# First block's entry: weight transfers issued earlier, column sums on TensorE, second group five units behind, attention's vector work first

## The chip, the cores and the metric

The kernel runs on one core of a Trainium2 chip. The time is device microseconds of one execution. The profile is of one execution; the times of the kernel before are of separate runs. In the rows PE is the matrix engine (TensorE), PEld its weight loads, DVE is VectorE, ACT is ScalarE, POOL is GpSimd, SP issues most of the transfers.

## The reference, cut to what matters

```python
# attention: B=4, 8 heads, 768 positions, head size 64; chunks of 32 queries,
# 16 keys to the left, 8 to the right, 8 memory tokens
a = np.exp(scores - max); a = a / (a.sum() + 1e-9); out = a @ v_full
x = out as [3072, 512]                  # 24 token tiles of 128
# first block (moe_*): one wide layer, d_ff = 2048
h = x @ w_in                            # 512 x 2048
r = np.maximum(h, 0.0)
g = s * (r * r) + b
x = g @ w_out                           # 2048 x 512
# second block (moe2_*): 8 experts, 384 tokens each, dealt out greedily by sorted gate logits
logits = x @ w_gate; ...; out[mask] = np.maximum(x[mask] @ w1[e], 0.0) @ w2[e]
```

Since g = s·r² + b, the first block is x2 = s·(r² @ w_out) + b·(sum of w_out over its 2048 rows). The kernel computes r² @ w_out and adds b times the column sums of w_out at the end of each tile; these column sums are what one part of the change moves to another engine.

## The kernel before, in words

Attention runs by token tile t (24 of them): `load_q`, `load_k`, `load_v` issue transfers, `k_transpose` and `stages` do the work (transposes pk and pq, scores sc, softmax on DVE and ACT, transposes pp, products po, the division `xr`, transposes px, and a split of the result into a rounded half and a remainder, `xT0` and `xT1`, kept for a group).

The first block runs by group j of two token tiles (256 columns) and by f, one of 16 slices of d_ff. One unit (j,f) is `gemm1` (12 products of 128x256 into a PSUM tile ph), then ACT's relu, square and rounding, then DVE's subtraction that leaves the remainder (line 324), then `gemm2` (6 products of 128x512 into the group's two accumulators). `gemm2` stands LAG = 3 units behind `gemm1`. The list `units` sets which unit follows which: ten units of group 0 first, then one of group 1 and one of group 0 in turn, then the rest of group 1, then groups 2 to 11 one after another.

The weights w_in and w_out of the first block arrive as 64-bit floats and are made into 32-bit ones on the chip, in 32 tiles of 128x512 (even numbers are slices of w_in, odd ones of w_out; the order is 0, 2, 4, 1, 6, 3, 8, 5 and so on). `convert` does one tile: a transfer of 512 KB into `raw` (3 buffers), ACT's y (line 277), DVE's u (278), u (280) and y (281), and in `split` ACT's rounding (262) and POOL's remainder (263). y and u have two buffers each. For a tile of w_out POOL then adds y into `wsum` (line 290). `load_wg`, between groups 1 and 2, multiplies a matrix of ones with wsum (pws, line 397), which sums over the partitions.

`begin` and `startup` write the order of SP's transfers by hand, and `begin` also that of TensorE. On the other engines, and later on TensorE too, a scheduler arranges the instructions when the kernel is built, in an order that then stands; each engine runs its own list in that order, and waits at an instruction until what it needs is there. A tile of w_in must be converted before `gemm1` of its f, one of w_out before `gemm2` of its f, and xT of group 1 must be there before any unit (1,f).

## Time and profile before

| | |
|---|---|
| median of 3 runs | 1113.73 us (1112.22 to 1116.49) |
| the profiled execution | 1110.14 us |
| its span | 1108.4 us |
| PE busy | 1017.7 us, 92% of the span |
| DVE busy | 776.3 us, 70% |
| ACT busy | 474.1 us, 43% |
| POOL busy | 230.9 us, 21% |

The span runs from the first to the last recorded instruction, and the execution's own time is 1.7 us longer. Busy shares are averages over stages with different limits: in the first 145 us the weights are converted while units already run, and from there to about 660 us the first block runs on. A row of the timeline gives an instruction's start, its length, engine, line, operation and the tiles it writes and reads; in square brackets stands the idle time before it and what ended that.

### The profile page before, as it was taken

How to read it: one execution, taken by the hardware profiler on the slowest of the kernel's cores; microseconds unless marked ns; L12 is line 12 of the kernel's file. 1: busy time of each engine (PE TensorE's matmuls, PEld its weight loads, DVE VectorE, ACT ScalarE, POOL GpSimd, SP SyncE). 2: the span in 40 equal slices, each digit the busy share in tenths (PEclk: the TensorE clock that was granted, in tenths of full speed). 3: DMA queues.
4: the chain of work that ended last, by engine and by line, in shares of the span. 5: the costliest groups of instructions: out<-in, count | busy, mean ns of one | idle time of the engine just before them, and what ended most of it. 6: DMA issues, size and time to landing. Idle time of an engine off the chain costs nothing.

```text
span 1108.4 us, 25066 instructions
## 1 busy us (share of the span) xinstructions
PE 1017.7 (92%) x9397; PEld 889.8 (80%) x9397; DVE 776.3 (70%) x2979; ACT 474.1 (43%) x1055; POOL 230.9 (21%) x257
## 2 busy tenths in 40 slices
PE   4678899999999999999999999958989899987997
PEld 3557788888888898989898888747878787877986
DVE  4898846984889598989698643579677667774210
ACT  4656554444444454545444445034244143333421
POOL 2566530000121011121120000010112020135631
PEclk9989999999999999999999998959999899998999
DMA  7966503121212121212211000144346063353500
GB/s 168 229 185 167 132 19 127 46 71 38 54 23 73 37 66 47 50 36 62 58 37 37 1 1 20 51 149 153 113 126 202 18 200 95 116 144 113 161 29 29
DMA packets 157913, 96.56 MB, mean 87 GB/s; under 512 B 100312, under 2 KB 141272, under 8 KB 157664
## 3 DMA queue, kind: packets, MB, share of 16 engines
q1 hardware_dynamic: 153376, 81.32, 27.2%
q0 software_dynamic: 3840, 12.59, 3.5%
q8 instruction: 74, 1.21, 0.5%
q10 hardware_dynamic: 576, 1.05, 0.3%
q14 instruction: 47, 0.39, 0.1%
HBM read 82.33 MB, written 12.60 MB: 86 GB/s over the span
## 4 chain that ended last, share of the span: by engine, by line
PE 63%; DVE 21%; issue 7%; DMA 5%; ACT 1%; POOL 1%; SPq 1%; POOLq 0%; DVEq 0%; ACTq 0%
PE ph L316 19%; PE o L345 19%; PE pg L910 8%; PE pf L889 7%; DVE lsc L378 5%; DVE e L839 4%; PE pc L708 2%; DVE u L280 2%; DMA raws<-in_moe_w_dram 2%; DVE g L324 1%; PE po L221 1%; PE sc L195 1%; DVE y L281 1%; DVE rounded L795 1%; PE px L870 1%
## 5 line engine op out<-in xcount | busy, mean ns | idle before, releaser
L316 PE MATMUL ph<-xT,win 128*128 128x256 f32 x2304 | 323.7, 288 | 10.0 <-ACT win L262 7.2
L316 PEld LDWEIGHTS ph<-xT,win 128*128 128x128 f32 x2304 | 301.6, 192 | 28.4 <-ACT win L262 10.6
L345 PE MATMUL o<-wout,g 128*128 128x512 f32 x1038 | 275.0, 400 | 4.4 <-DVE g L324 2.2
L345 PEld LDWEIGHTS o<-wout,g 128*128 128x128 f32 x1038 | 184.4, 189 | 39.4 <-DVE g L324 3.4
L378 DVE SCALAR_TENSOR_TENSOR lsc<-x,wgb 128x128 int8<-128x128 f32 x640 | 158.3, 299 | 3.3 <-DMA wgb<-wgd 1.1
L319 ACT ACTIVATE r<-ph 128x256 f32<-128x256 f32 x192 | 72.9, 382 | 172.0 <-PE ph L316 160.6
L889 PE MATMUL pf<-xgh,e 128*128 128x384 f32 x512 | 140.8, 349 | 0.0
L910 PE MATMUL pg<-e,hh 128*128 128x512 f32 x384 | 130.5, 415 | 0.0
L838 ACT ACTIVATE e<-raws 128x512 fp32r<-128x512 f32 x128 | 79.6, 630 | 93.8 <-DMA raws<-in_moe_w_dram 92.8
L324 DVE TENSOR_TENSOR g<-r,g 128x256 fp32r<-128x256 f32 x173 | 80.2, 465 | 53.7 <-ACT g L323 50.9
L889 PEld LDWEIGHTS pf<-xgh,e 128*128 128x128 f32 x512 | 96.5, 196 | 5.1 <-issue 3.0
L378 DVE SCALAR_TENSOR_TENSOR lsc<-c,wgb 128x512 int8<-128x512 f32 x128 | 98.9, 773 | 2.1
L910 PEld LDWEIGHTS pg<-e,hh 128*128 128x128 f32 x384 | 74.5, 198 | 19.1 <-issue 5.5
L889 PE MATMUL pf<-xgl,e 128*128 128x384 f32 x256 | 88.7, 346 | 0.0
L897 DVE SCALAR_TENSOR_TENSOR hl<-pf,hh 128x384 fp32r<-128x384 f32 x64 | 35.3, 553 | 69.0 <-ACT hh L896 69.0
L320 ACT ACTIVATE r<-r 128x256 f32<-128x256 f32 x192 | 79.7, 418 | 5.4
L910 PE MATMUL pg<-e,hl 128*128 128x512 f32 x192 | 79.4, 414 | 0.0
L323 ACT ACTIVATE g<-r 128x256 fp32r<-128x256 f32 x173 | 71.6, 416 | 5.0 <-PE o L345 0.3
L859 POOL DMA_INDIRECT xg<-x2d,vw x24 | 24.7, 1030 | 200.1 <-DVE vw L702 127.2
L917 POOL DMA_INDIRECT out_dram<-qk,vw x24 | 25.6, 1068 | 186.8 <-ACT qk L916 174.6
L839 DVE TENSOR_TENSOR e<-raws,e 128x512 fp32r<-128x512 f32 x96 | 60.2, 682 | 3.4 <-PE pg L910 1.3
L896 ACT ACTIVATE hh<-pf 128x384 fp32r<-128x384 f32 x64 | 30.9, 485 | 71.6 <-PE pf L889 70.2
(216 smaller groups left out, 1358.2 us busy)
## 6 DMA issues: line engine op xcount, KB each, us to landing
raws<-in_moe_w_dram SPq DMA_DIRECT2D x128, 256.0 KB
vw<-in_v_dram SPq DMA_DIRECT2D x176, 56.0 KB
raw<-in_moe_w_in_dram SPq DMA_DIRECT2D x16, 512.0 KB
raw<-in_moe_w_out_dram SPq DMA_DIRECT2D x16, 512.0 KB
k<-in_k_dram SPq DMA_DIRECT2D x24, 256.0 KB
q<-in_q_dram SPq DMA_DIRECT2D x24, 256.0 KB
x2d<-x SPq DMA_DIRECT2D x20, 256.0 KB
wgb<-wgd SPq DMA_DIRECT2D x1, 2048.0 KB
```

The costliest lines, as they stand in the source:

```text
L316: nc.tensor.matmul(ph, win_ap(a, kk, f), x[:, kk, :], start=(n == 0), stop=(n == 3 * KD - 1))
L319: nc.scalar.activation(r, ph, AF.Relu)
L320: nc.scalar.activation(r, r, AF.Square)
L323: nc.scalar.activation(hi, r, AF.Copy)
L324: nc.vector.tensor_tensor(lo, r, hi.bitcast(F32), op=ALU.subtract)
L345: nc.tensor.matmul(PO[j][u], g[:, u * P:(u + 1) * P], wout_ap(a, f), start=(f == 0 and n == 0), stop=(f == FT - 1 and n == 2))
L378: nc.vector.scalar_tensor_tensor(sc[:, z], a[:, z], 1.0, b[:, z], op0=ALU.mult, op1=ALU.mult, accum_out=acc[:, i:i + 1])
L838: nc.scalar.activation(hi, raw, AF.Copy)
L839: (V if ph < E - 2 else nc.gpsimd).tensor_tensor(lo, raw, hi.bitcast(F32), op=ALU.subtract)
L889: nc.tensor.matmul(pf, w[:, kk, f * P:(f + 1) * P], x[:, kk, :], start=(n == 0), stop=(n == 3 * KD - 1))
L897: V.scalar_tensor_tensor(lo, pf, 0.0, hi.bitcast(F32), op0=ALU.max, op1=ALU.subtract)
L910: nc.tensor.matmul(pg, h[:, j * P:(j + 1) * P], w[:, f, :], start=(n == 0), stop=(n == 3 * FT2 - 1))
```

## The change

Five things are changed, all before group 3. First, the transfers of the first three slices of w_in are issued earlier: the first before the memory tokens, the second before v of tile 0, the third between v of tiles 0 and 1. Second, POOL's clearing of wsum and its 16 additions are gone; TensorE multiplies a matrix of ones with both halves of each slice of w_out, 32 products of 128x512 into a PSUM tile psw (`column_sums`, two behind each `gemm2` of group 0), and the product with ones in `load_wg` is gone. Third, group 1 starts behind five units of group 0 and not ten. Fourth, the two PSUM banks that ph had until group 3 become one, `halves`, whose two halves are used in turn, and one for psw. Fifth, the DVE and ACT instructions of attention tiles 0 to 3 are marked as urgent for the scheduler. The conversions, which were all handed to the scheduler before the first unit, are now handed over two by two, ahead of each unit of group 0.

```diff
@@ -56,7 +56,6 @@
     b_col = const.tile([P, 1], F32, name="b_col")
     L = const.tile([P, E, NTILE], F32, name="L")
     wsum = const.tile([P, DM], F32, name="wsum")
-    nc.gpsimd.memset(wsum, 0.0)
 
     def bigw(shape, name):
         return big.tile([P] + shape, F32R, tag="w", name=name)
@@ -105,6 +104,20 @@
                                 mk[:B * M, 2 * hp:2 * hp + 2, :].rearrange("p h d -> p (h d)"),
                                 ident[:B * M, :B * M])
         nc.vector.tensor_copy(memkT.rearrange("p h b m -> p h (b m)"), pm[:, :, :B * M])
+
+    class Ahead:
+
+        def __init__(self, engine):
+            self.engine = engine
+
+        def __getattr__(self, name):
+            def call(*args, **kw):
+                with tc.high_priority():
+                    return getattr(self.engine, name)(*args, **kw)
+            return call
+
+    def engines(t):
+        return (Ahead(nc.vector), Ahead(nc.scalar)) if t < 2 * GT else (nc.vector, nc.scalar)
 
     vb = [None, None]
     q_raw, k_raw, kT, xT = {}, {}, {}, {}
@@ -152,21 +165,23 @@
                                           ap=[[D, r1 - r0], [2 * S * D, HP], [1, D]]))
 
     def k_transpose(t):
+        V, S = engines(t)
         x = k_raw.pop(t)
         pk = psa[0].tile([P, HP, P], F32, tag="pa", name=f"pk{t}")
         for hp in range(HP):
             nc.tensor.transpose(pk[:, hp, :], x[:, 2 * hp:2 * hp + 2, :].rearrange("p h d -> p (h d)"), ident)
         kT[t] = at.tile([P, HP, P], F32, tag="kT", name=f"kT{t}", bufs=3)
-        nc.scalar.activation(kT[t], pk, AF.Copy)
+        S.activation(kT[t], pk, AF.Copy)
 
     def windows(t):
...
@@ -257,10 +273,24 @@
 
     sctx = ExitStack()
     st = sctx.enter_context(tc.tile_pool(name="st", bufs=2))
+    onesr = st.tile([P, P], F32R, name="onesr", bufs=1)
+    nc.vector.tensor_scalar(onesr, ident, 0.0, 1.0, op0=ALU.mult, op1=ALU.add)
 
     def split(c, hi, lo, i):
         nc.scalar.activation(hi, c, AF.Copy)
         nc.gpsimd.tensor_tensor(lo, c, hi.bitcast(F32), op=ALU.subtract)
+
+    raws = {}
+
+    def fetch(src, a, n, i):
+        raw = st.tile([P, a, n, 2], I32, tag="raw", name=f"raw{i}", bufs=3)
+        nc.sync.dma_start(raw.rearrange("p a f w -> p a (f w)"),
+                          src.bitcast(I32).rearrange("(a p) f -> p a f", p=P))
+        return raw
+
+    def fetch_win(f):
+        if w_in.dtype != F32:
+            raws[2 * f] = fetch(w_in[:, f * P:(f + 1) * P], KD, P, 2 * f)
 
     def convert(src, a, n, hi, lo, i):
 
@@ -269,9 +299,7 @@
             nc.sync.dma_start(c, src.rearrange("(a p) f -> p a f", p=P))
             split(c, hi, lo, i)
             return c
-        raw = st.tile([P, a, n, 2], I32, tag="raw", name=f"raw{i}", bufs=3)
-        nc.sync.dma_start(raw.rearrange("p a f w -> p a (f w)"),
-                          src.bitcast(I32).rearrange("(a p) f -> p a f", p=P))
+        raw = raws.pop(i) if i in raws else fetch(src, a, n, i)
         y = st.tile([P, a, n], F32, tag="y", name=f"y{i}")
         u = st.tile([P, a, n], I32, tag="u", name=f"u{i}")
         nc.scalar.activation(y, raw[:, :, :, 1].bitcast(F32), AF.Copy, scale=2.0 ** -112)
@@ -286,8 +314,11 @@
         convert(w_in[:, f * P:(f + 1) * P], KD, P, win_ap3(0, f), win_ap3(1, f), 2 * f)
 
     def load_wout(f):
-        y = convert(w_out[f * P:(f + 1) * P, :], 1, DM, wout_ap3(0, f), wout_ap3(1, f), 2 * f + 1)
-        nc.gpsimd.tensor_tensor(wsum, wsum, y[:, 0, :], op=ALU.add)
+        convert(w_out[f * P:(f + 1) * P, :], 1, DM, wout_ap3(0, f), wout_ap3(1, f), 2 * f + 1)
+
+    def column_sums(f):
+        for a in range(2):
+            nc.tensor.matmul(psw[0], onesr, wout_ap(a, f), start=(f + a == 0), stop=(f == FT - 1 and a == 1))
 
     G = {}
 
@@ -307,8 +338,14 @@
             kept.append([k[:, 0], k[:, 1]])
         return (x[:, f % 4 + (4 if f >= 12 else 0), :] for x in kept[-1])
 
+    ps_h, half = None, [0]
+
     def gemm1(j, f):
-        ph = ps_h.tile([P, GN], F32, tag="ph", name=f"ph{j}_{f}")
+        if ps_h is None:
+            half[0] ^= 1
+            ph = halves[:, half[0], :]
+        else:
+            ph = ps_h.tile([P, GN], F32, tag="ph", name=f"ph{j}_{f}")
         xh, xl = xT[j]
         n = 0
         for kk in range(KD):
@@ -331,11 +368,11 @@
             pass
 
     def gemm2_(j, f):
-        nonlocal ps_o, ps_l
+        nonlocal ps_h, ps_o, ps_l
         if (j, f) == (3, 0):
             octx.close()
-            ps_o, ps_l = (actx.enter_context(tc.tile_pool(name=n, bufs=k, space=PSUM, reuse_waits="tile"))
-                          for n, k in (("ps_o3", 3), ("ps_l", 1)))
+            ps_h, ps_o, ps_l = (actx.enter_context(tc.tile_pool(name=n, bufs=k, space=PSUM, reuse_waits="tile"))
+                                for n, k in (("ps_h", 2), ("ps_o3", 3), ("ps_l", 1)))
         if f == 0:
             PO[j] = [ps_o.tile([P, DM], F32, tag="po", name=f"o{j}_{u}") for u in range(GT)]
         hi, lo = G.pop((j, f))
@@ -391,11 +428,7 @@
         nc.vector.tensor_tensor(wog[:, f, E:2 * E], wf, wog[:, f, 0:E].bitcast(F32), op=ALU.subtract)
 
     def load_wg():
-        ones = xp[0].tile([P, P], F32, tag="x2", name="onesP")
-        nc.vector.memset(ones, 1.0)
-        ps = psa[0].tile([P, DM], F32, tag="pa", name="pws")
-        nc.tensor.matmul(ps, ones, wsum, start=True, stop=True)
-        nc.vector.tensor_scalar(wsum, ps, b_col, None, op0=ALU.mult)
+        nc.vector.tensor_scalar(wsum, psw[0], b_col, None, op0=ALU.mult)
         wg[0] = xp[0].tile([P, E, DM], F32, tag="wgb", name="wgb", bufs=1)
         wgd = dram.tile([E, DM], F32, name="wgd")
         wr[0] = xp[0].tile([P, KD, E], F32, name="wr", bufs=1)
@@ -425,6 +458,7 @@
         load_q(0)
         load_k(1)
         k_transpose(1)
+        fetch_win(0)
         for i in range(2):
             load_mem(i, 0, nc.gpsimd.tensor_copy)
             vb[i] = 0
@@ -434,7 +468,9 @@
         next(run0)
         load_q(1)
         load_k(2)
+        fetch_win(1)
         load_v(0)
+        fetch_win(2)
         k_transpose(2)
         next(run1)
         load_v(1)
@@ -461,15 +497,17 @@
         with tc.manual_schedule(engines={mybir.EngineType.PE}):
             begin()
         ps_s.close()
-        psa[0], ps_h, ps_o = (
+        psa[0], ps_o, ps_w = (
             c.enter_context(tc.tile_pool(name=n, bufs=k, space=PSUM, reuse_waits="tile"))
-            for n, k, c in (("ps_a", 2, ctx), ("ps_h", 2, actx), ("ps_o", 4, octx)))
+            for n, k, c in (("ps_a", 2, ctx), ("ps_o", 4, octx), ("ps_w", 1, octx)))
+        psw = [ps_w.tile([P, DM], F32, name="psw")]
+        halves = ps_w.tile([P, 2, GN], F32, name="halves")
         startup()
-        feed(len(convs))
     gp = actx.enter_context(tc.tile_pool(name="gp", bufs=4, side="right", reuse_waits="tile"))
-    units = [(0, f) for f in range(10)]
+    SKEW = 5
+    units = [(0, f) for f in range(SKEW)]
     for f in range(FT):
-        units += [(1, f)] + ([(0, f + 10)] if f + 10 < FT else [])
+        units += [(1, f)] + ([(0, f + SKEW)] if f + SKEW < FT else [])
     units += [(j, f) for j in range(2, NG) for f in range(FT)]
     wog = twice = ps_l = wsum_g = None
 
@@ -506,11 +544,16 @@
             if i >= 4 * FT and i % 6 == 3 and gated < FT:
                 through_gate(gated)
                 gated += 1
+            if j == 0:
+                feed(2)
             gemm1(j, f)
             if j * FT + f < LATE:
                 pend.append((j, f))
             if pend and (len(pend) > LAG or j * FT + f >= LATE):
-                gemm2(*pend.pop(0))
+                gemm2(*pend[0])
+                z = pend.pop(0)
+                if z[0] == 0:
+                    column_sums(z[1])
             if j >= NG - 2 and f:
                 if f == 1:
                     twice = wr[0][0:2 * E, 0, :]
```

The first list is DVE's, at the place where xT of group 1 is completed (xT1_1<-px3, tile 3). u and y with a number are the conversions' tiles by that number, g1 is the remainder that `gemm2` needs, by group and f; a number behind the name only tells buffers apart. Before:

```order
L280 SCALAR_TENSOR_TENSOR u15_858<-y15_857,u15_858 128x512
L324 TENSOR_TENSOR g10_8_1227<-r0_8_1223,g00_8_1226 128x256
L281 SCALAR_TENSOR_TENSOR y15_857<-y15_857,u15_858 128x512
L280 SCALAR_TENSOR_TENSOR u20_869<-y20_868,u20_869 128x512
L241 TENSOR_TENSOR xT1_1_609<-px3_754,xT1_0_608 128x4x128
L278 TENSOR_SCALAR u17_879<-raw17_876 128x512
L281 SCALAR_TENSOR_TENSOR y20_868<-y20_868,u20_869 128x512
L278 TENSOR_SCALAR u22_890<-raw22_887 128x512
```

And in the changed kernel, where lines 278, 280, 281 and 324 have become 306, 308, 309 and 361, and line 116 is the wrapper of the urgent instructions:

```order
L116 TENSOR_TENSOR xr3_748<-po3_0_713,den3_747 128x4x64
L116 TENSOR_TENSOR xr3_748<-po3_1_714,den3_747 128x4x64
L308 SCALAR_TENSOR_TENSOR u17_1018<-y17_1017,u17_1018 128x512
L309 SCALAR_TENSOR_TENSOR y17_1017<-y17_1017,u17_1018 128x512
L308 SCALAR_TENSOR_TENSOR u22_1082<-y22_1081,u22_1082 128x512
L306 TENSOR_SCALAR u19_1092<-raw19_1089 128x512
L116 TENSOR_TENSOR xT1_1_610<-px3_754,xT1_0_609 128x4x128
L309 SCALAR_TENSOR_TENSOR y22_1081<-y22_1081,u22_1082 128x512
```

Before, tiles 17 and 22 begin behind this instruction; now tile 17 is done ahead of it, tile 22 lacks only its last step, and tile 19 has begun. The remainders of nine units of group 0 stand ahead of it before, and of five now.

The second list is DVE's at the end of the conversions, the last step of tile 31. Before:

```order
L206 TENSOR_REDUCE mx5_1682<-sc5_0_1647 128x4
L241 TENSOR_TENSOR xT2_1_1609<-px4_1603,xT2_0_1608 128x4x128
L207 TENSOR_TENSOR sm5_1681<-sc5_0_1647,mx5_1682 128x4x64
L280 SCALAR_TENSOR_TENSOR u31_1006<-y31_1005,u31_1006 128x512
L324 TENSOR_TENSOR g10_15_1840<-r0_15_1836,g00_15_1839 128x256
L324 TENSOR_TENSOR g11_6_1866<-r1_6_1862,g01_6_1865 128x256
L281 SCALAR_TENSOR_TENSOR y31_1005<-y31_1005,u31_1006 128x512
L205 MEMSET sc5_1_1648 32x4x8
```

And in the changed kernel:

```order
L308 SCALAR_TENSOR_TENSOR u29_1717<-y29_1716,u29_1717 128x512
L309 SCALAR_TENSOR_TENSOR y29_1716<-y29_1716,u29_1717 128x512
L308 SCALAR_TENSOR_TENSOR u31_1727<-y31_1726,u31_1727 128x512
L361 TENSOR_TENSOR g10_8_1261<-r0_8_1257,g00_8_1260 128x256
L309 SCALAR_TENSOR_TENSOR y31_1726<-y31_1726,u31_1727 128x512
L361 TENSOR_TENSOR g11_4_1286<-r1_4_1282,g01_4_1285 128x256
L361 TENSOR_TENSOR g10_9_1333<-r0_9_1329,g00_9_1332 128x256
L221 MEMSET sc5_0_1616 32x4x8
L222 TENSOR_REDUCE mx5_1651<-sc5_0_1616 128x4
```

Before, the remainders of 16 units of group 0 and 7 of group 1 stand ahead of the last step of tile 31, 23 in all; now it is 9 of group 0 and 4 of group 1, 13 in all, and the scores' maxima of tile 5 and the second half of xT2 stand behind it.

The third list is TensorE's, where group 1 begins (win and wout are the weights' halves, o the accumulators of `gemm2`, ph or halves the result of `gemm1`). Before:

```order
L345 MATMUL o0_1_1099<-wout00_78,g10_6_1175 128x512
L235 MATMUL px3_754<-ident_64,xr3_748 128x128 x4
L158 MATMUL pk5_1494<-ident_64,k5_1482 128x128 x4
L316 MATMUL ph0_9_1236<-xT0_0_420,win11_77 128x256
L316 MATMUL ph0_9_1236<-xT0_0_420,win01_75 128x256
...
L316 MATMUL ph0_9_1236<-xT0_0_420,win11_77 128x256
L316 MATMUL ph1_0_1262<-xT1_0_608,win00_74 128x256
L186 MATMUL pq4_1501<-ident_64,q4_1472 128x128 x4
L345 MATMUL o0_0_1098<-wout00_78,g00_7_1200 128x512
```

And in the changed kernel:

```order
L237 MATMUL po3_1_714<-vw1_95,pT3_711 32x65
L321 MATMUL psw_461<-wout10_79,onesr_106 128x512
L321 MATMUL psw_461<-wout00_77,onesr_106 128x512
L321 MATMUL psw_461<-wout10_79,onesr_106 128x512
L251 MATMUL px3_754<-ident_64,xr3_748 128x128 x4
L172 MATMUL pk5_1463<-ident_64,k5_1451 128x128 x4
L353 MATMUL halves_462<-xT1_0_609,win00_73 128x256
L321 MATMUL psw_461<-wout01_78,onesr_106 128x512
...
L353 MATMUL halves_462<-xT1_0_609,win10_75 128x256
L321 MATMUL psw_461<-wout11_80,onesr_106 128x512
L211 MATMUL sc4_0_1483<-kwin0_96,qT4_1475 32x64
```

Between units (0,4) and (1,0) there is now no `gemm1`, only products for psw and attention; before, unit (0,9) stands directly ahead of unit (1,0). From here on the changed list has `gemm2` one unit behind `gemm1` until group 3, and all 32 products for psw stand ahead of unit (1,6).

## Rows read from the trace of the kernel before

**Rows 1.** Windows of the span, one row a stretch; header first.

```profile
core 0: us, PE busy (x) PEld busy (x) DVE busy (x) ACT busy (x) POOL busy (x), PEclk, DMA share, GB/s
...
24.88:38.85 13.97, 3.79 (x16) 3.05 (x17) 12.20 (x27) 7.26 (x12) 6.52 (x5) 1.00 0.96 256
38.85:88.20 49.35, 39.75 (x454) 33.24 (x453) 45.01 (x74) 31.73 (x68) 30.13 (x23) 0.90 0.75 198
88.20:145.05 56.85, 50.51 (x471) 41.12 (x471) 50.05 (x69) 32.60 (x77) 36.98 (x32) 1.00 0.48 131
145.05:169.46 24.41, 24.41 (x212) 21.22 (x211) 7.89 (x21) 11.77 (x30) 4.80 (x7) 1.00 0.10 21
169.46:250.00 80.54, 80.28 (x867) 70.93 (x865) 69.37 (x463) 36.97 (x89) 3.81 (x13) 1.00 0.30 84
```

**Rows 2.** Chain of waits, 0 to 240 us: start, length, what.

```profile
20.27 8.92 DMA raw<-in_moe_w_out_dram
...
112.04 1.71 DVE u L280
...
132.64 1.97 PE ph L316 x14
...
161.35 1.40 PE o L345 x6
162.74 1.44 PE ph L316 x12
...
178.14 0.79 PE sc L195 x53
```

**Rows 3.** DVE by line, 0 to 168 us: busy us, mean ns, idle before.

```profile
L280 DVE SCALAR_TENSOR_TENSOR u<-y,u 128x512 int32<-128x512 int32 x32 | 34.3, 1071 | 9.7 <-ACT y L277 9.5
L281 DVE SCALAR_TENSOR_TENSOR y<-y,u 128x512 int32<-128x512 int32 x32 | 28.7, 896 | 1.5 <-DVE den L228 0.4
L278 DVE TENSOR_SCALAR u<-raw 128x512 int32<-128x512 int32 x32 | 23.3, 729 | 7.7 <-DMA raw<-in_moe_w_in_dram 6.4 <-DMA raw<-in_moe_w_out_dram 1.0
L324 DVE TENSOR_TENSOR g<-r,g 128x256 fp32r<-128x256 f32 x31 | 19.2, 630 | 12.5 <-ACT g L323 12.5
```

**Rows 4.** POOL timeline around 57 us: start, length, instruction.

```profile
56.70 1.46 POOL L290 TENSOR_TENSOR wsum<-wsum,y 128x512 f32<-128x512 f32 x1
58.12 1.46 POOL L263 TENSOR_TENSOR wout<-y,wout 128x512 fp32r<-128x512 f32 x1
```

**Rows 5.** DVE timeline around 60 us, the same columns.

```profile
56.94 1.50 DVE L278 TENSOR_SCALAR u<-raw 128x512 int32<-128x512 int32 x1
58.36 1.77 DVE L280 SCALAR_TENSOR_TENSOR u<-y,u 128x512 int32<-128x512 int32 x1
60.24 0.69 DVE L281 SCALAR_TENSOR_TENSOR y<-y,u 128x512 int32<-128x512 int32 x1
...
60.98 0.42 DVE L278 TENSOR_SCALAR u<-raw 128x512 int32<-128x512 int32 x1
...
63.67 0.41 DVE L324 TENSOR_TENSOR g<-r,g 128x256 fp32r<-128x256 f32 x1
```

**Rows 6.** ACT by line, first step of a conversion.

```profile
L277 ACT ACTIVATE y<-raw 128x512 f32<-128x512 f32 x32 | 21.4, 668 | 9.8 <-DMA raw<-in_moe_w_in_dram 4.5 <-POOL wout L263 2.9 <-POOL win L263 2.4
```

**Rows 7.** DVE timeline where the two groups' xT and the conversions end.

```profile
37.36 0.68 DVE L241 TENSOR_TENSOR xT<-px,xT 128x512 fp32r<-128x512 f32 x1
...
87.53 0.68 DVE L241 TENSOR_TENSOR xT<-px,xT 128x512 fp32r<-128x512 f32 x1
...
144.22 0.83 DVE L281 SCALAR_TENSOR_TENSOR y<-y,u 128x512 int32<-128x512 int32 x1
```

**Rows 8.** SP timeline: v of tiles 0 and 1.

```profile
9.34 8.88 SPq L150 DMA_DIRECT2D vw<-in_v_dram  x16
```

**Rows 9.** PE timeline between groups 1 and 2.

```profile
168.25 1.02 PE L397 MATMUL pws<-wsum,onesP 128*128 128x512 f32 x2
...
169.46 1.68 PE L316 MATMUL ph<-xT,win 128*128 128x256 f32 x12
```

More of the change, by code (lines that the diff above doesn't have):

```diff
@@ L159, in k_transpose @@
         kT[t] = at.tile([P, HP, P], F32, tag="kT", name=f"kT{t}", bufs=3)
-        nc.scalar.activation(kT[t], pk, AF.Copy)
+        S.activation(kT[t], pk, AF.Copy)
     def windows(t):
+        V, S = engines(t)
         b = t // TPB
@@ L180, in stages @@
     def stages(t):
+        V, S = engines(t)
         first, last = t % TPB == 0, t % TPB == TPB - 1
@@ L202, in stages @@
             if first:
[L203 removed]
+                V.memset(sc[par][0:CH, :, 0:LEFT], -1.0e30)
             if last:
[L205 to L207 removed]
+                V.memset(sc[par][P - CH:P, :, W - RIGHT:W], -1.0e30)
+            V.tensor_reduce(mx[:, par, :], sc[par], axis=AX.X, op=ALU.max)
+            V.tensor_tensor(sm[:, :, par, :], sc[par],
                                     mx[:, par, :, None].to_broadcast([P, HP, KW]), op=ALU.subtract)
[L209 removed]
+        S.activation(sm, sm, AF.Exp, scale=scale)
         pp = psa[0].tile([P, HP, P], F32, tag="pa", name=f"pp{t}")
@@ L239, in stages @@
         hi, lo = (xT[j][i][:, :, u * P:(u + 1) * P] for i in range(2))
-        nc.scalar.activation(hi, px, AF.Copy)
-        nc.vector.tensor_tensor(lo, px, hi.bitcast(F32), op=ALU.subtract)
+        S.activation(hi, px, AF.Copy)
+        V.tensor_tensor(lo, px, hi.bitcast(F32), op=ALU.subtract)
     def attention(t):
```

19 lines of the change are left out of this document (7 added, 12 removed).

## The prediction

> **What bounds the kernel now.** I read the stretches of the span first, then the chain of waits, then the groups by line, and last the timelines for the length of single instructions. The stretches [rows 1] show where time can be had: from 145.05 to 169.46 us TensorE (PE) is busy for 24.41 of 24.41 us, and to 250 us for 80.28 of 80.54, so behind 145 us nothing but PE's own work counts, and a delay at the entry is carried to the end. Ahead of that PE stands idle for 9.6 of 49.35 us between 38.85 and 88.20, and for 6.3 of 56.85 us up to 145.05, while VectorE (DVE) is busy for 45.0 and 50.1. In the first of these the granted clock averages 0.90, so part of PE's busy time there is work at less than full speed. The chain [rows 2] says the same in another way: in the entry it runs through a transfer of w_out (8.92 us) and through DVE's conversions (the one at 112.04, for instance), and from 132.64 on it is PE alone. DVE's conversions of the weights are what the entry waits for: three instructions on each of 32 tiles, 34.3 + 28.7 + 23.3 = 86.3 us, and another 19.2 us for the remainders of 31 units [rows 3]. Three marks on DVE's line set the pace: xT of group 0 is complete at 38.04 us, xT of group 1 at 88.21, and the last step of tile 31 ends at 145.05 [rows 7].
>
> **Part one, POOL's additions.** DVE's conversions take longer than they must. Beside POOL's addition at 56.70 (1.46 us) and the subtraction behind it at 58.12 [rows 4], DVE's shift takes 1.50 us and the next step 1.77; without a POOL instruction beside them the same shapes take 0.42 and 0.69, and the remainder 0.41 [rows 5]. Against the means of 1.071, 0.896, 0.729 and 0.630 us [rows 3] the excess is 32 x 0.38 = 12.2, 32 x 0.21 = 6.6, 32 x 0.31 = 9.9 and 31 x 0.22 = 6.8 us, 35.5 in all. It is shared by POOL's 48 instructions of this kind (16 additions, 32 subtractions), 0.74 us each. The 16 additions that go are thus worth 11.8 us of DVE by this mean. The bounds are nothing (POOL's subtractions then only meet other DVE instructions) and the whole addition, 16 x 1.46 = 23.4 us. I take the mean, since it comes from the same instructions. Also, ACT's first step waits 5.3 us for POOL [rows 6]; I take half of it, 2.6 us, as gone (bounds 0 and 5.3).
>
> [...]
>
> **Part two, the order of transfers.** The first three slices of w_in now come ahead of v of tiles 0 and 1, whose 16 issues keep SP for 8.88 us [rows 8]; v itself comes a little later, and tile 1 of the conversions, whose transfer takes 8.92 us [rows 2], goes out sooner. DVE waits 6.4 us in all for w_in's transfers [rows 3], so the gain lies between 0 and 6.4 us. The DMA engines are busy for 0.96 of the time from 24.88 to 38.85 [rows 1], so moving one transfer ahead mostly moves another back: I take 2.0 us, near the lower end. All loads of weights move with the queue, and they still wait for one of three buffers.
>
> **Part three, five units in place of ten, and attention first.** What counts is how much of PE's work stands behind the last conversion, because the conversions go through DVE in a fixed list with the remainders. Ahead of the last step of tile 31 DVE's list now has 13 remainders and not 23, and the second half of xT2 stands behind it: 10 x 0.63 + 0.68 = 7.0 us of DVE leave the stretch [rows 3, 7]. So tile 31 ends at 145.05 - 7.0 - 11.8 - 2.6 - 2.0 = 121.7 us.
>
> But then PE has these ten units still before it. After the last conversion the old kernel needs 24.41 us to group 2 [rows 1]. The new one needs besides this: ten units of 1.44 + 1.40 us [rows 2], 28.4; two more `gemm2`, since the lag is one there and not three, 2.8; some four of the new products for the column sums at 1.40 / 6 = 0.23 us, 0.9; the transposes and scores of tiles 6 and 7 that now stand ahead of group 2, for which I take 1.7 (0.79 for scores [rows 2], two sets of transposes at about half of that); less pws, 1.0 [rows 9]. Sum 57.2, so group 2 begins at 121.7 + 57.2 = 178.9 us. To compare, the old start at 169.46 [rows 9] has to get the 2.8 and the 1.7 added, work that the old kernel does later: 174.0. The change costs 4.9 us by this sum. The rest of the column sums (32 x 0.23 = 7.5 us less the four) is costed at nothing: PE is then waiting for xT1 or for DVE. If that cover were gone it would be 6.5 us.
>
> A check on another bound: xT of group 1. It stands behind about one and a half more conversions than before (a tile takes some 3.1 us: 2.7 for its three means, the rest for other work), but behind four remainders fewer, and with 5 us less of contention: 88.2 + 4.6 - 2.5 - 5 - 2.0 = 83.3 us. PE has no unit to do between (0,4) and (1,0), so it stands idle for about 20 us there, where the old kernel did five more units of 2.84 us. From 83.3 on 27 units remain, 76.7 us, with about 10 us of attention and column sums: 170.0, less than 178.9, so the conversions' end is the bound that decides. A clock lowered by the gap in PE's work (the mean of 0.90 in the row from 38.85 on) is in none of these sums.
>
> **Sum.** The profiled execution took 1110.14 us; with 4.9 us more it would be 1115.0. The median of the runs is 3.6 us above the profiled execution, so I forecast 1118.5 us, between unchanged and a little slower.
>
> **Rivals.** First: faster. If each addition holds DVE up for its whole 1.46 us, the additions are worth 23.4 us, tile 31 ends at 110.1 and group 2 begins at 167.3, 6.7 us sooner than 174.0: 1107; with DVE's waits for ACT (9.5 us in [rows 3]) going as well, down to 1101. For it speaks the pair at 56.70 and 56.94, where nearly the whole length shows as excess; against it the mean of 0.74. [...] Chance 0.22.
>
> Second: slower, the subtractions take the additions' place. POOL's 32 subtractions remain, and with less to do POOL runs them sooner and beside other DVE instructions; the row at 58.36 has one beside a subtraction, 1.77 us [rows 5]. Then the 11.8 us stay, tile 31 ends at 133.5 us, and group 2 begins 16.7 us late: 1130. It decides once less than a third of the excess goes; half of the loss gives 1124. Chance 0.14.
>
> Third: slower, one bank for two halves. In the changed list every `gemm1` up to group 3 waits for ACT's reading of the unit before it, and before of the one two back. ACT runs its list in order; where a conversion's step of 0.67 us [rows 6] stands ahead of that reading, PE waits. With 11 units ahead of the last conversion that is up to 7.4 us on top of my sum: 1126. [...] Behind the conversions a `gemm2` of 1.40 us lies between, which hides the reading. Chance 0.08.
>
> Fourth: the change does nothing that can be measured, since PE's lost work and DVE's gain cancel: 1113 to 1115. Chance 0.08.
>
> **How the numbers follow.** My own case (0.48) has its own range from 1112 to 1125. About 0.5% (5.6 us) is what a measurement can tell here from no change: faster is below 1108.2, slower above 1119.3. Of my case 0.27 lie within and 0.21 above. The first rival gives 0.20 to faster and 0.02 to no change, the second and third 0.22 to slower, the fourth 0.08 to no change. Sums: faster 0.20, same 0.37, slower 0.43. The range goes from 1103 to 1130: below, the strict contention with a part of DVE's waits; above, no gain from the additions.
>
> **What would show it.** In the new profile: DVE's steps should have means near 0.9, 0.8 and 0.6 us where 1.07, 0.90 and 0.73 stood; tile 31 should end at about 122 us (110 by the first rival, 134 by the second); xT1 at about 84; a gap in PE of some 20 us ahead of (1,0), with a lower granted clock behind it; and the first product of group 2 at about 179. I am wrong if tile 31 ends before 113 us or behind 128, or if PE behind it is not busy throughout.

## The result, and the profile after

The changed kernel takes 1128.28 us (median of 4 runs, 1125.32 to 1130.23), beside 1112.97 us of the kernel before on the same chip: 1.014 times as long, 95% interval 1.0116 to 1.0165, or 15 us lost. The forecast was 1118.5 us with 4.8 us lost: the sign held, the size was a third. The profiled execution has a span of 1123.5 us, 15.1 more than before.

The stretches of the changed kernel, cut at the same events as in [rows 1] (from xT0 complete to xT1 complete, to tile 31 done, to group 2 begins):

```profile
core 0: us, PE busy (x) PEld busy (x) DVE busy (x) ACT busy (x) POOL busy (x), PEclk, DMA share, GB/s
39.11:89.37 50.26, 35.34 (x398) 26.66 (x399) 44.64 (x77) 30.33 (x60) 21.32 (x18) 0.74 0.80 219
89.37:126.52 37.15, 33.14 (x308) 27.12 (x307) 33.37 (x51) 24.07 (x52) 19.03 (x18) 0.97 0.55 162
126.52:187.79 61.27, 61.27 (x549) 52.92 (x548) 17.22 (x40) 27.17 (x67) 6.66 (x15) 1.00 0.19 56
```

Between xT0 and xT1 TensorE is busy for 35.34 of 50.26 us at a mean clock of 0.74 (before: 39.75 of 49.35 at 0.90, with 60 more first products and 13 more second ones done). From xT1 to group 2 it takes 98.42 us; in [rows 1] the same way, 88.20 to 169.46, takes 81.26. These 17 us, and the 1.2 by which xT1 is later, are 18.3; some 4.5 of them are work that the old kernel does later (the second products and the attention that my sum set aside), which leaves about 14 us. The time shows 15, and an event far behind the entry, read below, 12.3.

The chain of waits of the changed kernel (start, length, what):

```profile
85.21 1.28 POOL win L281
...
87.74 0.69 DVE u L308
88.68 0.69 DVE xT L116
...
114.16 1.34 DVE u L308
...
119.65 0.42 DVE xr L247
...
121.74 1.43 PE halves L353 x12
123.40 1.40 PE o L382 x6
```

It passes through xT1 at 88.68, goes on through DVE's conversions to a step of attention (xr at 119.65) for which PE waits 2.8 us, and is PE's behind that, where [rows 2] had it from 132.64 on. By the chain alone DVE still seems to bind behind xT1; the runs below show how little that is worth.

DVE by line in the changed kernel, 0 to 190 us (the same columns as [rows 3]; lines 306, 308, 309, 361 for 278, 280, 281, 324):

```profile
L309 DVE SCALAR_TENSOR_TENSOR y<-y,u 128x512 int32<-128x512 int32 x32 | 29.6, 925 | 1.6
L308 DVE SCALAR_TENSOR_TENSOR u<-y,u 128x512 int32<-128x512 int32 x32 | 29.0, 905 | 5.9 <-ACT y L305 5.5
L306 DVE TENSOR_SCALAR u<-raw 128x512 int32<-128x512 int32 x32 | 18.8, 589 | 10.1 <-DMA raw<-in_moe_w_out_dram 5.1 <-DMA raw<-in_moe_w_in_dram 4.8
L361 DVE TENSOR_TENSOR g<-r,g 128x256 fp32r<-128x256 f32 x32 | 15.9, 497 | 34.8 <-ACT g L360 34.8
```

The conversion's three steps fell from 86.3 to 77.4 us, the remainders from 19.2 to 15.9: DVE did get faster, though the step at line 309 did not (896 ns before, 925 now). Of the 34.8 us that the remainders wait for ACT's copy, nearly all lie behind the last conversion; up to 126.52 us it is 1.0:

```profile
L361 DVE TENSOR_TENSOR g<-r,g 128x256 fp32r<-128x256 f32 x13 | 7.0, 536 | 1.0 <-ACT g L360 1.0
```

So up to the last conversion it is not ACT or PE that keeps DVE; behind xT1 it is busy for 33.37 of 37.15 us.

The three marks of [rows 7] in DVE's timeline of the changed kernel:

```profile
38.43 0.68 DVE L116 TENSOR_TENSOR xT<-px,xT 128x512 fp32r<-128x512 f32 x1
...
88.68 0.69 DVE L116 TENSOR_TENSOR xT<-px,xT 128x512 fp32r<-128x512 f32 x1
...
125.83 0.69 DVE L309 SCALAR_TENSOR_TENSOR y<-y,u 128x512 int32<-128x512 int32 x1
```

xT0 is complete at 39.11 us (38.04 before), xT1 at 89.37 (88.21), and tile 31 at 126.52 (145.05). The last mark came 18.5 us sooner, and yet group 2 begins 18.3 us later.

PE's timeline of the changed kernel (before xT1, at the first unit of group 1, a product for psw later, and group 2's first product, which answers to [rows 9]):

```profile
82.44 0.80 PE L321 MATMUL psw<-wout,onesr 128*128 128x512 f32 x1 [3.46 <-ACT wout L280]
...
89.84 2.28 PE L353 MATMUL halves<-xT,win 128*128 128x256 f32 x11
...
123.01 0.39 PE L321 MATMUL psw<-wout,onesr 128*128 128x512 f32 x1
...
187.79 1.60 PE L353 MATMUL halves<-xT,win 128*128 128x256 f32 x12
```

At 82.44 PE waits 3.46 us for a slice of w_out and then needs 0.80 us for one product for psw; at 123.01 the same product takes 0.39. Group 2 begins at 187.79, not at 178.9.

For comparing kernels I use one event far behind the entry, the transfer that writes the result of group 9, since the stretch behind it varies, from 505 to 512 us in the profiled executions of the kernels here (SP's timeline, before and then changed). Only one execution of each kernel was profiled, so such a mark has no interval.

```profile
601.74 1.14 SPq L365 DMA_DIRECT2D x2d<-x  x2
```

```profile
614.01 1.14 SPq L402 DMA_DIRECT2D x2d<-x  x2
```

By it the change costs 12.3 us; the other 2.8 us of the profiled difference arise behind it, and I have not traced them. PE between xT1 and this event, before and then changed, in the columns of [rows 1]:

```profile
88.21:601.74 513.53, 504.45 (x5320) 445.08 (x5320) 419.82 (x1902) 246.82 (x604) 96.84 (x135) 1.00 0.24 61
```

```profile
89.37:614.01 524.64, 518.45 (x5409) 458.62 (x5408) 408.80 (x1898) 252.10 (x613) 80.35 (x124) 1.00 0.22 57
```

PE is busy for 14.0 us more, on 89 more instructions, and idle for 2.9 us less; with the 1.2 by which xT1 is later, that is the 12.3.

### The profile page after: what moved, and what is told of

Read it like the earlier page. It is cut to its first block, busy times and chain, and to the rows that moved or that the text cites. A ratio compares the mean times of both kernels' runs of the same rounds, so it can differ in the third digit from the quotient of the medians.

```text
span 1123.5 us, 25101 instructions
## 1 busy us (share of the span) xinstructions
PE 1029.0 (92%) x9427; PEld 898.2 (80%) x9427; DVE 768.5 (68%) x2979; ACT 477.4 (42%) x1055; POOL 203.3 (18%) x240
## 4 chain that ended last, share of the span: by engine, by line
PE 64%; DVE 19%; issue 7%; DMA 6%; POOL 2%; ACT 1%; SPq 1%; POOLq 0%; DVEq 0%; ACTq 0%
PE o L382 20%; PE ph L353 15%; PE pg L953 8%; PE pf L932 7%; PE halves L353 5%; DVE lsc L415 5%; DVE e L882 4%; DMA raw<-in_moe_w_in_dram 3%; DMA raws<-in_moe_w_dram 2%; PE pc L751 2%; DVE u L308 2%; DVE y L309 1%; PE sc L211 1%; PE po L237 1%; DVE g L361 1%
## 5 line engine op out<-in xcount | busy, mean ns | idle before, releaser
L353 PE MATMUL ph<-xT,win 128*128 128x256 f32 x1680 | 231.4, 284 | 0.0
L353 PEld LDWEIGHTS ph<-xT,win 128*128 128x128 f32 x1680 | 218.3, 190 | 10.3
L932 PE MATMUL pf<-xgh,e 128*128 128x384 f32 x512 | 143.3, 355 | 0.0
L361 DVE TENSOR_TENSOR g<-r,g 128x256 fp32r<-128x256 f32 x173 | 76.8, 444 | 75.3 <-ACT g L360 74.9
L356 ACT ACTIVATE r<-ph 128x256 f32<-128x256 f32 x140 | 53.5, 382 | 137.6 <-PE ph L353 130.1
L932 PEld LDWEIGHTS pf<-xgh,e 128*128 128x128 f32 x512 | 98.4, 200 | 4.7 <-issue 2.5
L353 PE MATMUL halves<-xT,win 128*128 128x256 f32 x624 | 87.7, 290 | 1.4 <-ACT r L356 1.3
L353 PEld LDWEIGHTS halves<-xT,win 128*128 128x128 f32 x624 | 82.1, 195 | 5.8 <-ACT r L356 1.5
```

The costliest lines, as they stand in the source:

```text
L353: nc.tensor.matmul(ph, win_ap(a, kk, f), x[:, kk, :], start=(n == 0), stop=(n == 3 * KD - 1))
L356: nc.scalar.activation(r, ph, AF.Relu)
L361: nc.vector.tensor_tensor(lo, r, hi.bitcast(F32), op=ALU.subtract)
L932: nc.tensor.matmul(pf, w[:, kk, f * P:(f + 1) * P], x[:, kk, :], start=(n == 0), stop=(n == 3 * KD - 1))
```

## Experiments

All ratios are to the kernel before, on the same chip, with 95% intervals; a difference between two ratios carries both intervals.

**One part undone.** Ten units again:

```diff
-    SKEW = 5
+    SKEW = 10
```

> The changed kernel with group 1 behind ten units of group 0 again, all else as changed. If the five units are the cause (TensorE stands without units between (0,4) and xT1 at 89.4 us, then has 98 us of work), units (0,5) to (0,9) fill that gap: group 2 begins 10 to 14 us earlier, total about 1115 to 1118 us. If the column sums, the one bank or the transfers are the cause, the time stays within 3 us of 1128.

Measured: 1115.73 us, 1.0026 (1.0008 to 1.0044). The five units account for 1.14% (0.8 to 1.4%) or 12.7 us in the changed kernel. DVE's timeline of this run:

```profile
94.61 0.68 DVE L116 TENSOR_TENSOR xT<-px,xT 128x512 fp32r<-128x512 f32 x1
```

xT1 is 5.9 us later than in the changed kernel, and the event of group 9 still comes 9.4 us sooner (604.63): 60 more first products and 24 more second ones start ahead of xT1 by the trace, 12.8 us at 0.12 and 0.233 us each (1.44 / 12 and 1.40 / 6 by [rows 2]). So it is not xT1 alone that counts, but xT1 together with what PE still has to do behind it.

Attention not urgent:

```diff
-        return (Ahead(nc.vector), Ahead(nc.scalar)) if t < 2 * GT else ...
+        return (Ahead(nc.vector), Ahead(nc.scalar)) if t < 0 else ...
```

> The changed kernel without the urgency of attention's DVE and ACT instructions. Rival: the urgency pushes conversions back and makes the last of them (126.5 us) late; then without it tile 31 ends 3 to 6 us sooner and the total is about 1123. My theory: the urgency brings xT1 forward, so without it xT1 comes later than 89.4 and the total is 1128 to 1134.

Measured: 1.0147 (1.0105 to 1.019), as the changed kernel. xT1 is complete at 90.9 us and tile 31 at 130.2, so the urgency moved both a little. In the time it can't be seen; the event of group 9 is 4.6 us later here (618.60).

The three transfers back in their places:

```diff
-        fetch_win(0)
...
-        fetch_win(1)
         load_v(0)
-        fetch_win(2)
```

> The changed kernel with the first three transfers of w_in where they stood before. If the early transfers delay v and with it xT0 (39.1 us in place of 38.0), xT0 comes 1 to 3 us sooner and the total is 1125 to 1127. If they gain what I gave them (2 us), the total is 1130. My theory of the five units expects no more than 2 us either way.

Measured: 1118.0 us, 1.0059 (1.0036 to 1.0082). The early transfers cost 0.81% (0.5 to 1.1%), 9 us. xT0 comes 2.1 us sooner (36.98), as the expectation had it, but no theory of mine had the other 7 us. DVE's timeline of this run, and SP's at the event of group 9:

```profile
84.11 0.69 DVE L116 TENSOR_TENSOR xT<-px,xT 128x512 fp32r<-128x512 f32 x1
...
125.84 0.69 DVE L309 SCALAR_TENSOR_TENSOR y<-y,u 128x512 int32<-128x512 int32 x1
```

```profile
607.62 1.14 SPq L402 DMA_DIRECT2D x2d<-x  x2
```

xT1 comes 4.6 us sooner than in the changed kernel, tile 31 at the same 126.5 us, and the event of group 9 6.4 us sooner. That two kernels whose conversions end at the same time differ by this much was the first sign that this end doesn't decide. Behind xT1 the two differ by 1.8 us only.

All conversions handed over at once:

```diff
-            if j == 0:
-                feed(2)
...
+        feed(len(convs))
```

> The changed kernel with all conversions handed to the scheduler before the first unit, as in the kernel before. The order of conversions against remainders on DVE changes: more tiles ahead of the remainders. My theory expects little, 1125 to 1131, since TensorE's own work from xT1 on sets the end; if the handing over two by two is what sets the lag of one unit and the pace, the total falls to about 1120.

Measured: 1.0128 (1.0095 to 1.0162), within the interval of the changed kernel; this part is not the cause.

**One part alone.** The old kernel with five units:

```diff
-    units = [(0, f) for f in range(10)]
+    units = [(0, f) for f in range(5)]
```

> The kernel before with group 1 behind five units of group 0, nothing else changed. If the five units are the cause, this alone loses most of the 15 us: 1122 to 1128. If the column sums on TensorE or the one bank are, it stays at 1111 to 1116.

Measured: 1126.06 us, 1.0132 (1.0094 to 1.0171): this part alone loses 14.7 us (10 to 19). Stretches of this run up to xT1 (89.6 us) and behind it, in the columns of [rows 1]:

```profile
38.60:89.60 51.00, 33.77 (x393) 27.53 (x394) 47.80 (x72) 28.20 (x57) 29.94 (x24) 0.68 0.76 204
89.60:140.60 51.00, 42.22 (x305) 33.86 (x304) 44.88 (x56) 29.71 (x69) 32.31 (x26) 1.00 0.39 118
```

PE is busy for 33.8 of 51.0 us up to xT1 (39.75 of 49.35 before, but at a clock of 0.90 in place of 0.68), and xT1 comes no sooner than with ten units. How much work has moved behind xT1 is told by the products that start ahead of it, first products (line 316) and then second ones (line 345), before:

```profile
30.00:88.20 58.20, 21.52 (x121) 19.00 (x121) 0.91 0.77 201
30.00:88.20 58.20, 13.12 (x43) 7.89 (x44) 0.91 0.77 201
```

and in this run:

```profile
30.00:89.63 59.63, 12.89 (x73) 12.24 (x73) 0.65 0.78 206
30.00:89.63 59.63, 11.07 (x30) 6.28 (x30) 0.65 0.78 206
```

(PE's busy time and count, then PEld's.) These are 48 first products and 13 second ones fewer, 5.8 + 3.0 = 8.8 us at 0.12 and 0.233 us each, and not five whole units, 14.2 us: of its ten units the old kernel had done only seven to the end by xT1, since `gemm2` stands three units behind. At the event of group 9 this run is 14.2 us later (615.90), of which 1.4 are xT1, 9.3 are more busy time of PE behind it and 3.5 more idle time. That the loss equals five whole units is chance.

The old kernel without the additions:

```diff
-        nc.gpsimd.tensor_tensor(wsum, wsum, y[:, 0, :], op=ALU.add)
```

> The kernel before without POOL's 16 additions; the column sums are left out, so only the time counts. By the mean excess of 0.74 us an addition, DVE gains 11.8 us and the last conversion ends at about 133 us in place of 145; the total is then 4 to 11 us less (TensorE has 10 us of idle time to give back there). By whole instructions (23 us) tile 31 ends at 122 and TensorE binds: 10 us less. If the subtractions take the additions' place: no change, within 3 us of 1113.

Measured: 1101.93 us, 0.9914 (0.9884 to 0.9943): 9.6 us less. The last conversion ends at 128.6 us, 16.5 sooner, or 1.03 us an addition where I took 0.74; xT1 comes 3.1 us sooner (85.1).

The old kernel with one bank for ph:

```diff
+        halves = ps_w.tile([P, 2, GN], F32, name="halves")
...
-        ph = ps_h.tile([P, GN], F32, tag="ph", ...)
+        ph = halves[:, half[0], :]
```

> The kernel before with one bank of two halves for ph until group 3, nothing else changed. If the one bank costs by itself (the runs with and without it in the changed kernel differ by some 6 to 8 us), the time is 1117 to 1121. If it costs only where units of two groups follow the conversions closely, as with five units, it is within 3 us of 1113.

Measured: 1.0025 (1.001 to 1.0039), 2.8 us.

**Column sums and banks in the changed kernel.** Two of 32 products left:

```diff
-                if z[0] == 0:
-                    column_sums(z[1])
+                if z == (0, 0):
+                    column_sums(0)
```

> The changed kernel with 2 of the 32 products for the column sums left; the other 30 are left out. 30 x 0.23 = 7 us of TensorE go, of which 15 products (3.5 us) lie behind xT1, where TensorE binds. My theory: 1123 to 1126. Rival, column sums are the main cause (they wait for ACT in TensorE's list and hold up px behind them): 1118 or less.

Measured: 1124.66 us, 1.0128 (1.0082 to 1.0175). The other 30 products cost 0.1% with an interval from -0.4 to 0.6%, and 0.7 us at the event of group 9 (613.36). Then two banks for ph and no column sums:

```diff
-        psw = [ps_w.tile([P, DM], F32, name="psw")]
-        halves = ps_w.tile([P, 2, GN], F32, name="halves")
+        ps_h with 2 banks, as before
```

> The changed kernel with ph in two banks as before; the column sums are left out altogether. Beside the run with two products left it shows the one bank alone. If the wait for ACT's reading of the unit just before costs TensorE little (1.4 us of idle time in the profile), it is within 2 us of that run; if the one bank forces the lag of one and its waits, it is 4 to 8 us faster.

Measured: 1116.34 us, 1.0051 (1.003 to 1.0073), 0.8% below the run before it (interval 0.3 to 1.3%), with xT1 at the same 89.5 us. PE's waits in the run with two products and one bank, 89.5 to 250 us (what waited for what, total, times, longest):

```profile
PE o L382 <- DVE g L361: 3.1, 3, 1.5
```

With two banks the list has `gemm2` up to three units behind `gemm1`, where one bank has one, and this wait isn't there. But in the same window of the run with two banks another one stands in its place:

```profile
PE ph L354 <- ACT r L357: 2.9, 2, 2.4
```

All waits in the list together are 5.2 us with one bank and 4.5 with two, so waiting doesn't explain the difference. PE between xT1 and the event of group 9, with one bank and then with two, in the columns of [rows 1]:

```profile
89.53:613.36 523.83, 517.19 (x5394) 456.19 (x5395) 409.59 (x1899) 252.28 (x614) 81.40 (x123) 1.00 0.22 58
```

```profile
89.53:607.52 517.99, 512.09 (x5392) 455.00 (x5392) 410.41 (x1901) 251.64 (x614) 79.52 (x123) 1.00 0.23 58
```

Of the 5.8 us, 5.1 are busy time of PE on the same number of instructions within two, and 0.7 are idle time. I see more and shorter blocks in PE's list with one bank, and have no run that shows them to be the reason.

The same with the transfers late:

```diff
-        fetch_win(0)
...
-        fetch_win(1)
         load_v(0)
-        fetch_win(2)
```

> The changed kernel with ph in two banks, column sums left out, and the three transfers of w_in where they stood before. Against the run with two banks and early transfers (1.0051): if the early transfers cost what they do with one bank (9 us), 1106 to 1109; if their cost hangs on the one bank, within 3 us of 1117.

Measured: 1112.17 us, 1.001 (0.9989 to 1.0031). Here the early transfers cost 0.4% (0.1 to 0.7%), 4.6 us, where it was 9 us with one bank. The two intervals overlap, and at the event of group 9 they cost 5.6 us here (601.90 against 607.52) and 6.4 with one bank, so that the cost hangs on the bank isn't shown. Then only the first transfer early:

```diff
-        fetch_win(1)
         load_v(0)
-        fetch_win(2)
```

> The changed kernel with only the first transfer of w_in early (ahead of the memory tokens), the second and third behind v as before. If the two that stand ahead of and between v of tiles 0 and 1 do the harm, it is as without any of them, 1118 to 1121; if the first does it, by holding back the memory tokens and k of tile 2, it stays at 1126 to 1129.

Measured: 1123.15 us, 1.0126 (1.01 to 1.0152): the first transfer alone, ahead of the memory tokens, does most of the harm (0.67% above the run with none early, 0.3 to 1.0%). But xT1 is complete at 85.2 us here, 0.4 later than with none early, so the way by xT1 explains little of it. PE between xT1 and the event of group 9 in the run with none early and then in this one, and a stretch of this one behind xT1:

```profile
84.80:607.62 522.82, 517.27 (x5409) 457.08 (x5408) 410.64 (x1901) 253.90 (x615) 82.51 (x125) 1.00 0.23 59
```

```profile
85.25:614.09 528.84, 522.49 (x5410) 460.24 (x5411) 412.62 (x1904) 253.97 (x617) 83.30 (x125) 0.99 0.23 58
```

```profile
115.00:130.00 15.00, 12.56 (x67) 10.44 (x68) 11.26 (x19) 7.76 (x18) 7.88 (x6) 0.89 0.32 84
```

In the stretch PE is busy for 12.6 of 15 us at a clock of 0.89, where the run with late transfers has 15.0 at 1.00, and the last conversion ends at 130.3 us and not at 126.5. From xT1 to the event PE takes 6.0 us more: 0.8 idle and 5.2 busy on the same work (one instruction apart). By an estimate from the granted clock (0.93 from 85 to 100 us, 0.89 from 115 to 130), at most 2.7 of the 5.2 are the lower clock; the rest is open. DVE does its work in another order in the two runs; how a transfer that is earlier by 4 us leads to that, I can't say.

**Which of the two bounds.** The two long DVE steps left out, for nine tiles at the end or for six ahead of xT1:

```diff
+        if i not in (22, 24, 25, 26, 27, 28, 29, 30, 31):    # the second run: (13, 15, 16, 17, 18, 20)
             nc.vector.scalar_tensor_tensor(u, yi, 3, u, ...)
             nc.vector.scalar_tensor_tensor(yi, yi, -2 ** 31, u, ...)
```

> The changed kernel with the two long DVE steps of a conversion left out for the last nine tiles (22 and 24 to 31), so only the time counts; some 18 of them, at 0.9 us 16 us of DVE behind xT1. As my prediction had it (the end of the conversions decides), the end comes 10 us or more sooner: 1117 or less. By the rival that the runs so far suggest (xT1 and TensorE's own work from there on decide; tile 31 ends at 126 to 127 us in four kernels whose ends differ by 9 us), xT1 stays at about 89.4 and the end moves by 0 to 4 us, the idle time that TensorE still has behind xT1: 1124 to 1128.

> The changed kernel with the two long DVE steps left out for six tiles that stand ahead of xT1 (13, 15, 16, 17, 18, 20), so only the time counts; 12 of them, some 11 us of DVE. If xT1 decides, it comes 8 to 11 us sooner (about 80) and so does the end: 1118 to 1120. If the end of the conversions decides, it does so too, by 11 us; the pair with the run on the last nine tiles tells the two apart.

Measured: the first 1125.78 us, 1.0116 (1.008 to 1.0152); the second 1119.2 us, 1.0048 (1.003 to 1.0066). DVE's timeline and SP's event of group 9, of the first run:

```profile
88.30 0.68 DVE L116 TENSOR_TENSOR xT<-px,xT 128x512 fp32r<-128x512 f32 x1
...
112.85 0.48 DVE L306 TENSOR_SCALAR u<-raw 128x512 int32<-128x512 int32 x1 [2.50 <-DMA raw<-in_moe_w_out_dram]
```

```profile
612.45 0.36 SPq L403 DMA_DIRECT2D x2d<-x  x1
```

and of the second:

```profile
84.20 0.68 DVE L116 TENSOR_TENSOR xT<-px,xT 128x512 fp32r<-128x512 f32 x1
...
121.15 0.69 DVE L310 SCALAR_TENSOR_TENSOR y<-y,u 128x512 int32<-128x512 int32 x1
```

```profile
608.67 1.14 SPq L403 DMA_DIRECT2D x2d<-x  x2
```

In the first, DVE's last conversion step (line 306, the only one that is left for tile 31) ends at 113.3 us, 13.2 sooner, and the event of group 9 comes 1.6 us sooner. In the second, xT1 comes 4.5 us sooner, the conversions end 4.7 us sooner, and the event 5.3 us sooner. The second moves both, so it tells them apart only beside the first, and beside the run with late transfers, which moves xT1 alone: the changed kernel follows xT1, and not the end of the conversions. The run with only the first transfer early is the exception; there PE's work behind xT1 itself takes longer. The whole time of the second run is 0.9% (0.6 to 1.2%) or 10 us below the changed kernel's, while the two profiled executions differ by 4.2 us, and I can't place the rest. (The six tiles brought xT1 half of the 8 to 11 us that I expected; I have not traced why.)

**Towards a faster kernel.** Ten units and late transfers together:

```diff
-    SKEW = 5
+    SKEW = 10
...
-        fetch_win(0)
...
-        fetch_win(1)
-        fetch_win(2)
```

> The changed kernel with ten units again and the transfers of w_in where they stood: column sums on TensorE with one bank, conversions handed over two by two, and attention's urgency stay. If the two losses add (12.7 and 9 us from the runs with one of them undone), the total is 1106 to 1108, 4 to 6 us below before. If both act through the same wait for xT1, and ten units fill that, the transfers' part is gone already: 1112 to 1116.

Measured: 1114.43 us, 1.0004 (0.9985 to 1.0022): the losses don't add. With ten units xT1 is again 5.2 us sooner for the late transfers (90.05), but the event of group 9 only 1.9 (602.70). If urgency and feeding cost nothing here either, the gain from the additions must be cancelled by column sums and one bank; no run shows this apart. Then the old kernel with the additions replaced by products in two parts, and two banks:

```diff
-        nc.gpsimd.tensor_tensor(wsum, wsum, y[:, 0, :], op=ALU.add)
+                if z[0] == 0 and z[1] < 10:     # in an accumulator bank, before group 1 takes it
+                    column_sums(early_sums[0], 0, 10, z[1])
...
+                for ff in range(10, FT):        # between groups 1 and 2
+                    column_sums(ps, 10, FT, ff)
```

> The kernel before with POOL's additions replaced by products on TensorE, with two banks for ph kept: ten slices are summed behind their second products in an accumulator bank that group 1 does not need yet, the other six (12 products, 2.8 us) between groups 1 and 2. Leaving the additions out gave 9.6 us; the 12 products take back 2.8, less 0.9 for the product with ones, the first 20 (4.7 us) lie mostly in TensorE's idle time: 1104 to 1108. If products in TensorE's list hold up attention's transposes behind them by waiting for w_out, 1110 to 1114.

Measured: 1106.38 us, 0.994 (0.9917 to 0.9963): 6.7 us faster than the kernel before, and than the changed one by 2%. Its stretches (to xT1, and to 126.6 us, just behind the last conversion), the two marks on DVE, and SP's event:

```profile
38.00:85.70 47.70, 42.07 (x477) 35.53 (x477) 44.27 (x80) 33.93 (x74) 23.01 (x18) 1.00 0.81 226
85.70:126.60 40.90, 37.47 (x283) 31.62 (x282) 37.82 (x53) 27.06 (x61) 18.87 (x17) 1.00 0.51 143
```

```profile
85.03 0.68 DVE L240 TENSOR_TENSOR xT<-px,xT 128x512 fp32r<-128x512 f32 x1
...
124.12 1.79 DVE L282 SCALAR_TENSOR_TENSOR y<-y,u 128x512 int32<-128x512 int32 x1
```

```profile
593.67 1.14 SPq L371 DMA_DIRECT2D x2d<-x  x2
```

PE is busy for 42.07 of 47.70 us ahead of xT1 at a clock of 1.00, xT1 is complete at 85.7 us, and group 9 is out 8.1 us sooner than before. With five units in it, and its two parts of the sums cut there:

```diff
-    units = [(0, f) for f in range(10)]
+    units = [(0, f) for f in range(5)]
...
-                for ff in range(10, FT):
+                for ff in range(5, FT):
```

> The fast variant (column sums on TensorE in two parts, two banks) with group 1 behind five units in place of ten; five slices are summed early and eleven between groups 1 and 2, ten products or 2.3 us more there. If the five units cost 12 us also where additions, bank and transfers are not in play: 1118 to 1122. If they hurt only together with those: 1108 to 1112.

Measured: 1115.95 us, 1.0056 (1.0033 to 1.0078). The five units cost 1.16% (0.8 to 1.5%) or 12.9 us here too, where neither additions nor one bank nor early transfers are in play.

## Why the prediction was wrong in size

**The step that failed** is the check on xT1: "From 83.3 on 27 units remain, 76.7 us, with about 10 us of attention and column sums: 170.0, less than 178.9, so the conversions' end is the bound that decides." Both of its sizes were off. xT1 came at 89.4, and the work behind it took 98.4 us, not 86.7; so this bound is 187.8, above the other, which with the measured 126.5 + 57.2 is 183.7. PE by line in the changed kernel, 89.37 to 187.79 us, busy us and mean:

```profile
L353 PE MATMUL halves<-xT,win 128*128 128x256 f32 x323 | 44.7, 288 | 0.0
L382 PE MATMUL o<-wout,g 128*128 128x512 f32 x156 | 43.0, 403 | 0.3 <-DVE g L361 0.3
L321 PE MATMUL psw<-wout,onesr 128*128 128x512 f32 x15 | 5.6, 415 | 0.0
```

From start to start, the 27 units take 42.0 us for the first products and 41.9 for the second (those of 26 units): 83.9 and not 76.7, with 4.0 us of waits, 3.7 of them for attention's tiles 4 and 5, and the slow first unit in it. Column sums (4.0) and attention with the gate (10.3) take 14.3, not 10. xT1 itself was missed by the term for the transfers: with them in their old places it comes at 84.8 us, and the check without its 2.0 us for them has 85.3. (Its 5 us less of contention had no row of its own; without the additions xT1 came 3.1 us sooner in the old kernel.)

Neither of the two signs that were named for being wrong showed it: tile 31 ended at 126.5, between 113 and 128, and PE was busy throughout behind it. What showed it were xT1 (89.4, not 84) and the first product of group 2 (187.8, not 179). That the measured 1128 stands beside the 1130 of the second rival and the 1126 of the third is chance; the runs bear out the mechanism of neither.

**The five units** were seen and not charged to xT1. "PE stands idle for about 20 us there" is near: from 66 us to xT1 PE has no unit and is idle for 11 of 23 us. Alone they cost 14.7 us, in other company 12.7 and 12.9. I let the earlier end of the conversions pay for it, and that end was not the bound. Nor is it five units of 2.84 us that move: it is 8.8 us of products in the old kernel, and the rest is idle time behind xT1 and a later xT1.

**The transfers** had the wrong sign: a gain of 2.0 us was put in, bounded by nothing below; 9 us were lost with one bank and 4.6 with two. This is the term whose lower end should have been below zero: the DMA engines stood at 0.96, and I wrote myself that moving one ahead moves another back. That is what SP's timeline of the changed kernel shows. The first transfer of w_out, which I had going out sooner, goes out later than the 20.27 us of [rows 2], and v of tiles 0 and 1 is issued from 11.59 to 21.12 us in place of 9.34 to 18.22:

```profile
22.15 0.37 SPq L287 DMA_DIRECT2D raw<-in_moe_w_out_dram  x1
```

**The additions** were right in kind and too small: 11.8 us of DVE were forecast, 16.5 measured at the last conversion and 9.6 in the time of the old kernel. The first rival, with DVE held up for the whole of each addition, has 1.46 us an addition [rows 4]; the run gives 1.03, between that and the mean of 0.74 that I took. The second rival (the subtractions take the additions' place) had no gain at all, and is refuted by it.

**The one bank** stood as a rival at 7.4 us and 0.08. It costs 2.8 us alone and 0.8% (0.3 to 1.3%) in the changed kernel, but not by the wait for ACT's reading that I priced, which is 1.3 us in the changed kernel (ahead of the products at 56.27, behind ACT's reading of the unit before them, 55.85 to 56.22). With ten units that wait is 4.2 us ahead of xT1. A wait of `gemm2` for the remainder shows in the run with two products (3.1 us) and hardly in the changed kernel (0.3), and two banks have a wait of 2.9 us in its place. What the bank costs there is busy time of PE, 5.1 us of 5.8, and why the same products take longer stays open.

**Column sums at nothing** held within what was measured, 0.1% (-0.4 to 0.6%), though 15 of the 32 products, 4.0 us, stand behind xT1, where PE binds; the urgency and the feeding held too.

Taken together: five units +12.9, additions -9.6, one bank +2.8, transfers +4.6 to +9.0 give +10.7 to +15.1 us, beside 15 measured. The parts lean on one another, so this isn't a proof: without units and transfers the sum has -6.8 us, where the run with ten units and late transfers has +0.4. What each does through its list remains open for the transfers and for the bank.

## What to carry to other kernels

When a matrix engine fills the span, ask at each event that it waits for how much of its work could have run ahead of that event; what moves from ahead of the wait to behind it is paid for, however much faster the other engine gets (here the conversions ended 18.5 us sooner, and group 2 began 18.3 us later). Count the instructions that are really done ahead of the event: here 8.8 us of products moved and not the 14.2 of five units, and the rest of the loss was waiting. Where two bounds stand some microseconds apart in a forecast (here 9), work out the second as carefully as the first, with every piece of attention and every slow start in it. A transfer moved ahead on a full queue needs a price below zero: here three of them cost 9 us with one bank and 4.6 with two, and the DMA engines of the kernel before stood at 0.96 from 24.88 to 38.85 us.
